# State products on half of the rows, and 64- and 32-wide attention tiles

## The chip, the core and the metric

One core of a Trainium2 chip runs the whole program in one launch. The metric is the device time in microseconds (us); smaller is better. Before the change the median of 3 runs is 1411.97 us (1411.93 to 1413.6). The profile is of one further execution, which took 1415.93 us.

## The reference

Three stages follow each other. `B, H, S, Ns, D` are 8, 8, 512, 32, 64: batches, heads, tokens, state rows of a head, and the width of a head. `x` and `state` are drawn in fp32, the weights are stored in 64 bits.

```
scores = scale * x @ state.T              # per batch and head: 512 x 32
a      = softmax(scores);   xread = a @ state
scores2 = scale * state @ x.T             # 32 x 512
a2     = softmax(scores2);  sread = a2 @ x
tokens = concat([xread, sread]) -> (8*(512+32)) x 512
h  = ((tokens @ w1) * (tokens @ w2)) @ w3
y  = h @ w_out
out = (sigmoid(y @ w_gate) * (y @ w_val)) @ w_out2
```

Since `xread = a @ state`, the product `xread @ w1` is `a @ (state @ w1)`: the kernel multiplies each head's state with its 64 rows of `w1` and `w2` once, and then uses `a` as the only moving operand of the first feed-forward layer. These state products, the scores and `sread` are what the change touches.

## The kernel before

**Number formats.** Weights arrive as 64-bit words (tile `raw`, 512 KB a load). ScalarE (ACT) and VectorE (DVE) turn them into fp32 (tile `m`, lines 87 to 101). A product of full accuracy is made of three fp32r matmuls: an operand is split into a high part (ACT, line 61) and a low part (DVE or GpSimd (POOL), line 66), and `products` (line 103) issues high by high, and both mixed products. Scores and `sread` use plain fp32 operands instead, and the trace has two matmuls for each such call.

**State products.** The state lies in `bd`, transposed, as block-diagonal pieces: 128 rows are the 64 dimensions of two neighbouring heads, and 128 columns are 2 batches x 2 heads x 32 state rows, half of them zeros by the block structure. `z` (line 285) is filled with zeros, four DMAs on SyncE's queue (SP) put the state in, 16 transposes and four copies make `bd`. `state_split` (line 304) makes the high and low parts `bds`. A `sw_step` (line 337) takes one 128 x 512 block `wh` of `w1` or `w2`, and makes 2 x 3 matmuls into two PSUM tiles `psw`; ACT copies them to `swst` and stores them to `swd` in DRAM. There are 32 steps, in two passes of 16: the first pass is the head of the program (the columns for the first half of the batches); the second, for the other half, is spread over the first layer of t = 1 and t = 2.

**The main loop over t.** Each of the eight t takes one batch (`ffn1`, line 408). Slots 0 to 7 each make a pair of 128 x 512 products `pab` from `a` (tiles `aT`) and `swh`, the split of what `sw_weights` (line 458) reads back from `swd`; slots 8 to 11 make the product `py` with `wp = w3 @ w_out`. Before a slot's matmuls the functions hung into it run: `after` holds the rest of the attention of this batch (`a2t`, `sread`, `sreadt`, lines 231 to 269), `before` the attention of the next batch (`xt`, `scores`, softmax). `w_out`, `w3` and `wp` are prepared in t = 0, so that the stretch has more DVE work.

**What sets the order.** TensorE (PE) runs in the order in which the code is written. The other engines are put in order by a scheduler at build time. `ps_at`, the PSUM pool of the attention, has two buffers, and `psw` uses the four of `ps_main`.

**After 620 us** the second feed-forward stage runs; the change does not touch it.

Of the kernel before, what the change touches and what calls it, by code (L numbers as in the profile page):

```python
# [20 lines left out]
def tile_state_attention__then__gated_ffns(  # L21
# [20 lines left out]
    P = 128  # L42
# [75 lines left out]
    sw_d = dram.tile([2, 2, 2, 2, P, B // 2, 512], F32, name="swd")  # L118
# [19 lines left out]
    bd = keep.tile([P, G, B // 2, P], F32, name="bd")  # L138
# [7 lines left out]
    with tc.manual_schedule(engines={mybir.EngineType.PE}):  # L146
# [13 lines left out]
        def attention(b):  # L160

            b2, bp = divmod(b, B // 2)
# [14 lines left out]
            def scores():  # L177
                t["st"] = at.tile([P, 2, SC * 4, NS], F32, name="st")
                t["e2"] = at.tile([P, 2, S], F32, name="e2")
                m2 = at.tile([P, 2], F32, name="m2")  # L180
                s2 = at.tile([P, 2], F32, name="s2")
                t["r2"] = at.tile([P, 2], F32, name="r2")
                for k in range(2):
                    pt = ps_at.tile([P, 512], F32, tag="at", name="psc")
                    for q in range(2):
                        nc.tensor.matmul(
                            pt[64 * q : 64 * q + 64],
                            bd[:, 2 * k + q, bp, b2 * 64 : b2 * 64 + 64],
                            t["xT"][:, 2 * k + q],
                            start=True,  # L190
                            stop=True,
                        )
                    nc.vector.transpose(out=t["st"][:, k].rearrange("p a n -> p (a n)"), in_=pt)
# [46 lines left out]
            def sread():  # L240
                pt = ps_at.tile([P, 2, P], F32, tag="at", name="psr")
# [10 lines left out]
                t["sr"] = at.tile([P, 2, P], F32, name="sr")  # L252
# [5 lines left out]
            def sreadt():  # L258
                pt = ps_at.tile([P, 2, 2, 2, NS], F32, tag="at", name="psrt")
                for k in range(2):  # L260
                    nc.tensor.transpose(
                        pt[:, k].rearrange("p q h n -> p (q h n)"), t["sr"][:, k], ident
                    )
                xv = p2["xst"].rearrange("p (k q) n -> p k q n", q=2)
                for h2 in range(2):
                    nc.vector.tensor_copy(
                        out=xv[64 * h2 : 64 * h2 + 64, :, :, b * NS : (b + 1) * NS],
                        in_=pt[64 * h2 : 64 * h2 + 64, :, :, h2],
                    )
# [15 lines left out]
        z = p1.tile([P, B // 2, G, 2, D], F32, name="z", bufs=1)  # L285
        nc.vector.memset(z, 0.0)
        for b2 in range(2):
            for h2 in range(2):
                p0 = b2 * 64 + h2 * 32
                nc.sync.dma_start(  # L290
                    out=z[p0 : p0 + NS, :, :, h2, :].rearrange("p b g d -> p (b g) d"),
                    in_=state[b2 * (B // 2) : (b2 + 1) * (B // 2), h2::2].rearrange(
                        "b g n d -> n (b g) d"
                    ),
                )
        for g in range(G):
            pt = ps_main.tile([P, 512], F32, tag="m", name="pt")
            for bp in range(B // 2):
                nc.tensor.transpose(
                    pt[:, bp * P : (bp + 1) * P], z[:, bp, g].rearrange("p a d -> p (a d)"), ident  # L300
                )
            copy("act", bd[:, g].rearrange("p a b -> p (a b)"), pt)

        def state_split(pool, bp0):
            t = [pool.tile([P, G, 2, P], F32R, name=f"bds{i}", bufs=1) for i in range(2)]
            for g in range(G):
                split(t[0][:, g], t[1][:, g], bd[:, g, bp0 : bp0 + 2])
            return t
# [12 lines left out]

        def sw_prep(pool, cvs, save):
            def prep(i):
                c, g = (0, 2, 1, 3)[i // G], i % G
                a, hf = divmod(c, 2)
# [11 lines left out]
        def sw_step(i, bp0, bds, wh, pool):  # L337
            c, g = (0, 2, 1, 3)[i // G], i % G
            a, hf = divmod(c, 2)
            st = pool.tile([P, 2, 512], F32, name="swst", bufs=3 if bp0 == 0 else 2)  # L340
            po = [ps_main.tile([P, 512], F32, tag="m", name="psw") for _ in range(2)]
            products(*[(po[q], [([t[:, g, q] for t in bds], wh)]) for q in range(2)], late=1)
            for q in range(2):
                copy("act", st[:, q], po[q])
            nc.scalar.dma_start(out=sw_d[hf, g % 2, g // 2, a, :, bp0 : bp0 + 2], in_=st)

        order = [q * (B // 2) + bp for bp in range(B // 2) for q in range(2)]
        before, after = attention(order[0])
        bds = state_split(p1, 0)
# [4 lines left out]
        for i in range(2 * JF):  # L354
            sw_step(i, 0, bds, wh(i), p1)
            if i == 0:
                for fn in stages:
                    fn()
        p1.release()
# [98 lines left out]
        def sw_weights(b):  # L458
            b2, bp = divmod(b, B // 2)

            def prep(j):
                f = pb.tile([P, 2, 2, P], F32, tag="swf", name="swf", bufs=3)
                f0 = j % 4 * P
                for q in range(2):
                    nc.sync.dma_start(
                        out=f[64 * q : 64 * q + 64].rearrange("p k a f -> p (k a) f"),
                        in_=sw_d[
                            j // 4, q, :, :, 64 * b2 : 64 * b2 + 64, bp, f0 : f0 + P
                        ].rearrange("k a p f -> p (k a) f"),
                    )  # L470
# [5 lines left out]
                return [[t[i][:, :, a] for i in range(2)] for a in range(2)]  # L476
# [25 lines left out]
        def after_wp():  # L502
# [7 lines left out]
            p2["bds"] = state_split(p2["sw"], 2)  # L510
# [100 lines left out]
        for t, b in enumerate(order):  # L611
# [11 lines left out]
            if 1 <= t <= 2:  # L623
                for i in range(JF):
                    slots[i + 3].append(
                        lambda i=i + (t - 1) * JF: sw_step(i, 2, p2["bds"], p2["wh"](i), p2["sw"])
# [508 lines left out]
```

## Time and profile before

| | us |
|---|---|
| median of 3 runs | 1411.97 |
| the profiled execution | 1415.93 |
| its span | 1414.2 |
| PE busy (matmuls) | 1343.5 |
| weight loads (PEld) | 1145.6 |
| DVE busy | 924.7 |
| ACT busy | 750.2 |
| POOL busy | 278.3 |

PE is busy for 95% of the span, but not evenly: the table of 40 slices on the page shows 5 to 6 tenths in the first two slices (35 us each), 9 in nearly all from the fifth slice on. A busy PE isn't one at its peak, since a matmul's latency counts as busy: what a stretch costs is read from the times at which one group follows the other in the chain that ended last. [...]

### The profile page before, as it was taken

Reading aid. Unit: us, or ns where it says so; the run is one execution under the profiler, and the core shown is the slowest. Engines: PE = TensorE matmul, PEld = TensorE weight load, DVE = VectorE, ACT = ScalarE, POOL = GpSimd, SP = SyncE. Lnnn points to the kernel's source line nnn. Section 1 sums busy time; section 2 is a strip of 40 time slices with the busy share of each in tenths; the row PEclk is TensorE's granted clock in tenths of the full one; section 3 lists DMA queues with packets and bytes.
Section 4 is the critical chain, followed back from the end, with each engine's and each line's share of the span. In section 5 each row is a group of like instructions: output and inputs, shape, how many; then the busy total and the mean of one; then the engine's idle time right before and its main releaser. Section 6 shows DMA issues by size and latency. Waiting matters only on the chain.

```text
span 1414.2 us, 18988 instructions
## 1 busy us (share of the span) xinstructions
PE 1343.5 (95%) x6560; PEld 1145.6 (81%) x6560; DVE 924.7 (65%) x1523; ACT 750.2 (53%) x1480; POOL 278.3 (20%) x255
## 2 busy tenths in 40 slices
PE   5669999999998999999999999999999999999997
PEld 3348877777876777898988998988988888988996
DVE  6789756645555566528677667778777677556543
ACT  6877656756445456436546546545545544433421
POOL 2352113324334234001121121021121110000000
PEclk9889999999999999999999999999999999999999
DMA  9867637754446354383343347655445694134132
GB/s 264 290 195 212 199 135 230 228 195 127 138 119 164 90 155 152 118 319 116 133 151 100 117 165 285 239 183 169 136 167 184 227 324 159 62 108 137 49 104 67
DMA packets 169128, 237.18 MB, mean 168 GB/s; under 512 B 46920, under 2 KB 111944, under 8 KB 166984
## 3 DMA queue, kind: packets, MB, share of 16 engines
q1 hardware_dynamic: 130536, 163.15, 36.6%
q10 hardware_dynamic: 37344, 63.39, 12.8%
q0 software_dynamic: 1152, 9.44, 1.9%
q8 instruction: 51, 0.84, 0.2%
q14 instruction: 45, 0.37, 0.1%
HBM read 150.99 MB, written 84.93 MB: 167 GB/s over the span
## 4 chain that ended last, share of the span: by engine, by line
PE 80%; DVE 6%; issue 5%; DMA 4%; POOL 2%; ACT 2%; ACTq 0%; SPq 0%; DVEq 0%; POOLq 0%
PE po L1019 19%; PE psA L922 18%; PE psB L922 9%; PE pab L112 8%; PE py L112 7%; PE psC L922 5%; PE pab L115 4%; PE py L115 4%; DMA yf<-yd 2%; PE pwp L112 2%; POOL wh L66 2%; PE pwp L115 1%; PE psr L245 1%; PE pxt L170 1%; DMA raw<-in_moe_w 1%
## 5 line engine op out<-in xcount | busy, mean ns | idle before, releaser
L922 PE MATMUL psA<-y,wt 128*128 128x448 f32 (+1 forms) x1440 | 304.6, 360 | 5.6 <-ACT u L61 2.8
L922 PEld LDWEIGHTS psA<-y,wt 128*128 128x128 f32 x1440 | 266.3, 188 | 25.8 <-ACT u L61 3.9
L1019 PE MATMUL po<-wo,p 128*128 128x512 f32 x1224 | 280.7, 389 | 0.4 <-DVE p L590 0.4
L1019 PEld LDWEIGHTS po<-wo,p 128*128 128x128 f32 x1224 | 229.5, 188 | 48.3 <-DVE p L590 1.0
L922 PE MATMUL psB<-y,wt 128*128 128x448 f32 (+1 forms) x720 | 161.1, 359 | 0.0
L66 POOL TENSOR_TENSOR o<-m,o 128x256 fp32r<-128x256 f32 x72 | 59.3, 823 | 503.3 <-ACT o L61 449.1
L112 PE MATMUL pab<-aT,swh 128*128 128x512 f32 x512 | 145.7, 407 | 12.2 <-ACT asb L61 4.7
L922 PEld LDWEIGHTS psB<-y,wt 128*128 128x128 f32 x720 | 133.5, 188 | 8.5
L112 PE MATMUL py<-u,wp 128*128 128x512 f32 (+1 forms) x576 | 132.2, 381 | 2.1 <-DVE u L66 1.7
L61 ACT ACTIVATE u<-psA 128x448 f32<-128x448 f32 (+1 forms) x120 | 63.9, 532 | 127.7 <-PE psA L922 103.0
L112 PEld LDWEIGHTS py<-u,wp 128*128 128x128 f32 x576 | 104.0, 189 | 28.5 <-issue 5.7
L66 POOL TENSOR_TENSOR swh<-swf,swh 128x512 fp32r<-128x512 f32 x64 | 90.8, 1424 | 167.9 <-ACT swh L61 155.0
L112 PEld LDWEIGHTS pab<-aT,swh 128*128 128x128 f32 x512 | 95.3, 193 | 35.0 <-ACT asb L61 6.4
L61 ACT ACTIVATE p<-sg 128x448 fp32r<-128x448 f32 (+1 forms) x120 | 67.9, 566 | 86.6 <-DVE sg L958 79.0
L434 DVE TENSOR_TENSOR asb<-asb,pab 128x512 f32<-128x512 f32 (+1 forms) x72 | 47.0, 654 | 98.8 <-PE pab L115 90.3
L101 DVE CUSTOM_DVE_ANT_0 m<-m,r 128x1024 uint16<-128x1024 uint16 (+1 forms) x116 | 80.1, 692 | 11.1 <-ACT r L90 1.3
L66 DVE TENSOR_TENSOR u<-asb,u 128x512 fp32r<-128x512 f32 (+1 forms) x72 | 65.9, 916 | 30.7 <-ACT u L61 30.1
L1034 DVE TENSOR_TENSOR ob<-po,ob 128x512 f32<-128x512 f32 x68 | 46.8, 688 | 58.7 <-PE po L1019 55.4
L115 PE MATMUL pab<-aT,swh 128*128 128x512 f32 x256 | 81.7, 401 | 2.0 <-POOL swh L66 2.0
L922 PE MATMUL psC<-y,wt 128*128 128x448 f32 (+1 forms) x360 | 80.9, 360 | 1.1 <-DVE s L955 1.1
L61 ACT ACTIVATE y<-yf 128x448 fp32r<-128x448 f32 (+1 forms) x120 | 63.1, 558 | 32.4 <-DMA yf<-yd 32.4
L98 DVE SCALAR_TENSOR_TENSOR m<-raw,m 128x512 uint32<-128x512 uint32 (+1 forms) x116 | 78.2, 676 | 3.2
(118 smaller groups left out, 2028.3 us busy)
## 6 DMA issues: line engine op xcount, KB each, us to landing
raw<-in_moe_w SPq DMA_DIRECT2D x48, 512.0 KB, 5.6
wt<-wd SPq DMA_DIRECT2D x12, 1792.0 KB, 7.6
part<-ob SPq DMA_DIRECT2D x68, 256.0 KB, 2.8
ob<-part SPq DMA_DIRECT2D x68, 256.0 KB, 3.9
yf<-yd SPq DMA_DIRECT2D x37, 448.0 KB, 4.0
swd<-swst ACTq DMA_DIRECT2D x32, 512.0 KB, 4.1
swf<-swd SPq DMA_DIRECT2D x128, 128.0 KB, 3.7
wd<-o ACTq DMA_DIRECT2D x56, 256.0 KB, 2.3
```

Source lines behind the costliest of these rows:

```text
L61: return nc.scalar.activation(out=o, in_=i, func=AF.Copy)
L66: (sub or nc.vector).tensor_tensor(out=lo, in0=src, in1=hi.bitcast(F32), op=ALU.subtract)
L98: nc.vector.scalar_tensor_tensor(out=mu, in0=hi, scalar=0x80000000, in1=mu, op0=ALU.bitwise_and, op1=ALU.bitwise_or)
L101: nc.vector.tensor_tensor(out=m.bitcast(I32), in0=m.bitcast(I32), in1=r, op=ALU.add)
L112: nc.tensor.matmul(o, w[i], xx[k], start=n == 0 and i + k == 0, stop=False)
L115: nc.tensor.matmul(o, w[1 - late], xx[late], start=False, stop=n == len(pairs) - 1)
L170: nc.tensor.transpose(pt[:, c * P : (c + 1) * P], xn[b][:, g, c].rearrange("p a d -> p (a d)"), ident)
L245: nc.tensor.matmul(pt[64 * q : 64 * q + 64, k], t["a2"][:, k, c, 64 * q : 64 * q + 64], xn[b][:, 2 * k + q, c].rearrange("p a d -> p (a d) ...
L434: p2["dve"] = nc.vector.tensor_tensor(out=asb[:, :n], in0=asb[:, :n], in1=pab[1][:, :n], op=ALU.mult)
L922: nc.tensor.matmul(o, w[:, i, kb * P : (kb + 1) * P], xx[kb][h], start=start, stop=i == 1 and kb == 1, skip_group_check=True,)
L1019: nc.tensor.matmul(o, pt[j][i][:, s * P : (s + 1) * P], wot[j][:, h], start=j == js[0] and i + h == 0, stop=j == js[-1] and i == 1,)
L1034: nc.vector.tensor_tensor(out=ob, in0=o, in1=ob, op=ALU.add)
```

## The change

`bd` is replaced by `stT`, the plain transpose of the state: 128 rows are the dimensions of a pair of heads (even head in rows 0 to 63, odd head in rows 64 to 127), and the columns of pair `g` are 8 batches x 32 state rows. No zeros are stored.

- **State products**: the stationary operand of one matmul is 64 rows x 128 columns (four batches x 32 state rows of one head). A step makes 3 x 2 matmuls again, `k` = 0 on rows 0 to 63 into one PSUM tile, `k` = 1 on rows 64 to 127 into the other. The number of steps (32) and of matmuls (192) stays.
- **Scores**: 8 calls instead of 4, each on 64 rows and 32 columns; the two halves `k` go to two PSUM tiles that are both taken at the start.
- **sread**: 32 calls instead of 16, each on 128 rows and 32 columns with 64 moving columns instead of 128.
- **sreadt**: one transpose and one copy instead of two of each.
- **Head**: no zero fill; eight state DMAs, six of them on ACT's queue; 4 transposes and one copy before the first step, the other 4 and one copy after the fifth.
- **DRAM layout** of `swd`: a store writes two runs of 2 KB for each partition instead of one of 4 KB; one DMA of 256 KB instead of two of 128 KB reads a slot's block back. Batches are taken in the order 0 to 7.

```diff
-    sw_d = dram.tile([2, 2, 2, 2, P, B // 2, 512], F32, name="swd")
+    sw_d = dram.tile([2, 2, G, NS, 4, 2, 2, 512], F32, name="swd")
-    bd = keep.tile([P, G, B // 2, P], F32, name="bd")
+    stT = keep.tile([P, G, NSR], F32, name="stT")
...
-                for k in range(2):
-                    pt = ps_at.tile([P, 512], F32, tag="at", name="psc")
-                    for q in range(2):
+                pts = [ps_at.tile([P, 512], F32, tag="at", name="psc") for _ in range(2)]
+                for g in range(G):
+                    for k in range(2):
                         nc.tensor.matmul(
-                            pt[64 * q : 64 * q + 64],
-                            bd[:, 2 * k + q, bp, b2 * 64 : b2 * 64 + 64],
-                            t["xT"][:, 2 * k + q],
+                            pts[k][NS * g : NS * g + NS],
+                            stT[64 * k : 64 * k + 64, g, b * NS : (b + 1) * NS],
+                            t["xT"][64 * k : 64 * k + 64, g],
...
-                        for q in range(2):
+                        for g in range(G):
                             nc.tensor.matmul(
-                                pt[64 * q : 64 * q + 64, k],
-                                t["a2"][:, k, c, 64 * q : 64 * q + 64],
-                                xn[b][:, 2 * k + q, c].rearrange("p a d -> p (a d)"),
+                                pt[NS * g : NS * g + NS, k],
+                                t["a2"][:, k, c, NS * g : NS * g + NS],
+                                xn[b][:, g, c, k],
...
-        z = p1.tile([P, B // 2, G, 2, D], F32, name="z", bufs=1)
-        nc.vector.memset(z, 0.0)
...
+        z = p1.tile([P, 2, H, D], F32, name="z", bufs=1)
+        for b in range(B):
+            (nc.sync if b in (1, 3) else nc.scalar).dma_start(
+                out=z[b % 4 * NS : b % 4 * NS + NS, b // 4],
+                in_=state[b].rearrange("h n d -> n h d"),
+            )
...
+        def state_split(pool, h4):
+            t = [pool.tile([P, G, P], F32R, name=f"sts{i}", bufs=1) for i in range(2)]
+            for g in range(G):
+                v = [i[:, g].rearrange("p (n b) -> p b n", b=4) for i in t]
+                split(*v, stT[:, g, h4 * P : (h4 + 1) * P].rearrange("p (b n) -> p b n", b=4))
+            return t
...
-            products(*[(po[q], [([t[:, g, q] for t in bds], wh)]) for q in range(2)], late=1)
+            for m, (x, w) in enumerate(((0, 0), (1, 0), (0, 1))):
+                for k in range(2):
+                    nc.tensor.matmul(
+                        po[k],
+                        sts[x][64 * k : 64 * k + 64, g],
+                        wh[w][64 * k : 64 * k + 64],
+                        start=m == 0,
+                        stop=m == 2,
+                    )
```

On PE, in slot 4 of t = 1 (`psr` is `sread`, `psw` a state step, `pab` the first layer; in a row the calls stand, the width of the output's partitions x its columns), before:

```order
L115 MATMUL pab<-aT_1665,swh_1737 128x512 x2
L245 MATMUL psr<-xn,a2tr 64x128 x16
L112 MATMUL psw<-wh_1819,bds_1487 128x512
L112 MATMUL psw<-wh_1819,bds_1488 128x512
L112 MATMUL psw<-wh_1819,bds_1487 128x512
L112 MATMUL psw<-wh_1819,bds_1488 128x512
L115 MATMUL psw<-wh_1820,bds_1487 128x512 x2
L112 MATMUL pab<-aT_1665,swh_1770 128x512
```

and now:

```order
L115 MATMUL pab<-aT_1667,swh_1738 128x512 x2
L246 MATMUL psr<-xn,a2tr 32x64 x32
L344 MATMUL psw<-wh_1819,sts_1490 128x512 x2
L344 MATMUL psw<-wh_1819,sts_1491 128x512 x2
L344 MATMUL psw<-wh_1820,sts_1490 128x512 x2
L112 MATMUL pab<-aT_1667,swh_1770 128x512
```

The place of the groups is the same; `psr` has twice the calls, and the six calls of `psw` now alternate between the two row halves, while they went tile by tile before.

On PE, in slot 8 of t = 1 (`psc` are the scores of the next batch, `py` the second product), before:

```order
L115 MATMUL pab<-aT_1665,swh_1981 128x512 x2
L112 MATMUL psw<-wh_2020,bds_1487 128x512
L112 MATMUL psw<-wh_2020,bds_1488 128x512
L112 MATMUL psw<-wh_2020,bds_1487 128x512
L112 MATMUL psw<-wh_2020,bds_1488 128x512
L115 MATMUL psw<-wh_2021,bds_1487 128x512 x2
L186 MATMUL psc<-xT,bd 64x512 x4
```

and now:

```order
L115 MATMUL pab<-aT_1667,swh_1994 128x512 x2
L344 MATMUL psw<-wh_2031,sts_1490 128x512 x2
L344 MATMUL psw<-wh_2031,sts_1491 128x512 x2
L344 MATMUL psw<-wh_2032,sts_1490 128x512 x2
L185 MATMUL psc<-xT,stT 32x512 x8
```

The scores have eight calls instead of four, right behind a state step.

On ACT, from the start of the program, before:

```order
L89 ACT_TABLE_LOAD
L89 ACTIVATE m<-raw 128x512
L90 ACTIVATE r<-raw 128x512
L89 ACTIVATE m<-raw 128x512
L90 ACTIVATE r<-raw 128x512
L61 ACTIVATE wh_151<-m 128x512
L61 ACTIVATE wh_164<-m 128x512
L61 ACTIVATE bd<-pt 128x512
L89 ACTIVATE m<-raw 128x512
L61 ACTIVATE bd<-pt 128x512
L61 ACTIVATE bds_132<-bd 128x256 x2
L61 ACTIVATE bd<-pt 128x512 x2
```

and now:

```order
L282 DMA z<-in_state 32x8x64 x6
L61 ACT_TABLE_LOAD
L61 ACTIVATE stT<-pt 128x4x128
L89 ACTIVATE m<-raw 128x512
L61 ACTIVATE sts_117<-stT 128x4x32 x4
L90 ACTIVATE r<-raw 128x512
L89 ACTIVATE m<-raw 128x512
L90 ACTIVATE r<-raw 128x512
L89 ACTIVATE m<-raw 128x512
L61 ACTIVATE wh_136<-m 128x512
```

Six DMA issues come first, the state's copy and its four halved splits stand ahead of the weights' conversion instead of behind it, and three of the four `bd` copies are gone from this place (one comes back after the fifth step).

## Rows read from the trace of the kernel before

**Rows 1.** The page, part 1: busy time and share of each engine.

```profile
PE 1343.5 (95%) x6560; PEld 1145.6 (81%) x6560; DVE 924.7 (65%) x1523; ACT 750.2 (53%) x1480; POOL 278.3 (20%) x255
```

**Rows 2.** Busy time of each engine by stretch (stretch, its length, engines, clock, DMA).

```profile
core 0: us, PE busy (x) PEld busy (x) DVE busy (x) ACT busy (x) POOL busy (x), PEclk, DMA share, GB/s
...
40.00:70.00 30.00, 21.56 (x57) 12.43 (x57) 20.89 (x26) 24.38 (x46) 12.71 (x10) 0.81 0.88 296
70.00:110.00 40.00, 27.75 (x112) 19.68 (x113) 34.01 (x41) 28.91 (x53) 21.63 (x16) 0.83 0.70 197
...
190.00:330.00 140.00, 137.89 (x677) 110.21 (x676) 80.60 (x110) 87.14 (x159) 42.16 (x31) 1.00 0.57 183
330.00:440.00 110.00, 108.52 (x570) 86.89 (x569) 62.60 (x87) 59.20 (x106) 42.17 (x35) 1.00 0.47 140
```

**Rows 3.** The chain that ended last, in t = 3 (start, length, what).

```profile
333.49 1.90 PE psr L245 x32
335.38 1.12 PE pab L112 x4
...
336.97 0.91 PE pab L112 x4
...
341.06 0.22 PE psrt L261 x2
...
349.44 1.87 PE psc L186 x8
351.31 3.89 PE py L112 x16
...
357.02 3.63 PE py L112 x16
```

**Rows 4.** The same chain in t = 1, a state step.

```profile
215.46 0.91 PE psw L112 x4
216.37 0.45 PE psw L115 x2
```

**Rows 5.** Weight loads in order of time around one batch's scores (start, length, what).

```profile
511.64 0.14 PEld L186 LDWEIGHTS psc<-xT,bd 128*64 128x64 f32 x2 [0.28 <-issue]
512.07 0.14 PEld L186 LDWEIGHTS psc<-xT,bd 128*64 128x64 f32 x2 [0.29 <-issue]
```

**Rows 6.** All matmuls of scores and of sread (durations in ns: least, median, most).

```profile
L186 PE MATMUL psc<-xT,bd x64: 592/592/643, 19.6 to 512.5; 128*64 128x512 f32 x64
...
L245 PE MATMUL psr<-xn,a2tr x256: 272/273/476, 107.4 to 548.6; 128*64 128x128 f32 x128
```

**Rows 7.** ACT in order of time in the head's steady part.

```profile
55.20 0.63 ACT L61 ACTIVATE wh<-m 128x512 fp32r<-128x512 f32 x1 [0.58 <-DVE m L101]
...
56.85 1.08 ACT L61 ACTIVATE swst<-psw 128x512 f32<-128x512 f32 x2
```

**Rows 8.** All engines in order of time, the first 15 us.

```profile
0.74 0.87 SPq L80 DMA_DIRECT2D raw<-in_moe_w  x2
...
3.03 1.93 SPq L290 DMA_DIRECT2D z<-in_state  x4
...
11.57 0.60 ACT L61 ACTIVATE bd<-pt 128x512 f32<-128x512 f32 x1 [0.50 <-PE pt L299]
...
13.09 0.72 ACT L61 ACTIVATE bds<-bd 128x256 fp32r<-128x256 f32 x2
...
13.74 1.53 PE L112 MATMUL psw<-wh,bds 128*128 128x512 f32 x4
```

**Rows 9.** The chain in t = 1, from the scores to the next slots.

```profile
231.12 1.03 PE psc L186 x4
...
256.21 6.30 DMA raw<-in_moe_w
...
269.94 1.20 PE pab L112 x4
```

**Rows 10.** The chain in t = 5, a pause of PE.

```profile
445.07 5.88 issue
```

More of the change, by code (lines that the diff above doesn't have):

```diff
@@ L251, in sread @@
                             )
-                t["sr"] = at.tile([P, 2, P], F32, name="sr")
+                t["sr"] = at.tile([P, 2, D], F32, name="sr")
                 for k in range(2):
@@ L258, in sreadt @@
             def sreadt():
[L259 to L269, printed above, removed]
+                pt = ps_at.tile([P, G, NS], F32, tag="at", name="psrt")
+                nc.tensor.transpose(
+                    pt.rearrange("p g n -> p (g n)"), t["sr"].rearrange("p k d -> p (k d)"), ident
+                )
+                nc.vector.tensor_copy(out=p2["xst"][:, :, b * NS : (b + 1) * NS], in_=pt)
             before = {
@@ L284, in tile_state_attention__then__gated_ffns, with state_turn @@
         tc.swap_default_side()
-        z = p1.tile([P, B // 2, G, 2, D], F32, name="z", bufs=1)
-        nc.vector.memset(z, 0.0)
[L287 to L294, printed above, removed]
-                )
[L296 to L308, printed above, removed]
+        z = p1.tile([P, 2, H, D], F32, name="z", bufs=1)
[4 more added lines that the diff above has]
+            )
+        def state_turn(h4):
+            pt = ps_main.tile([P, 512], F32, tag="m", name="pt")
+            for g in range(G):
+                nc.tensor.transpose(
+                    pt[:, g * P : (g + 1) * P],
+                    z[:, h4, 2 * g : 2 * g + 2].rearrange("p a d -> p (a d)"),
+                    ident,
+                )
+            copy("act", stT[:, :, h4 * P : (h4 + 1) * P], pt.rearrange("p (g m) -> p g m", g=G))
+        state_turn(0)
         def ahead(prep, depth, count):
@@ L320, in ahead, with sw_tile @@
             return take
+        def sw_tile(i):
+            hf, r = divmod(i, 2 * G)
+            return (hf, *divmod(r, 2))
         def sw_prep(pool, cvs, save):
             def prep(i):
-                c, g = (0, 2, 1, 3)[i // G], i % G
-                a, hf = divmod(c, 2)
+                hf, g, a = sw_tile(i)
                 wf = cvt((w1, w2)[a][g * P : (g + 1) * P, hf * 1024 : (hf + 1) * 1024], cvs[i % len(cvs)])
@@ L335, in sw_prep, with sw_step @@
             return ahead(prep, 2, 2 * JF)
[L337 to L340, printed above, removed]
-            po = [ps_main.tile([P, 512], F32, tag="m", name="psw") for _ in range(2)]
-            products(*[(po[q], [([t[:, g, q] for t in bds], wh)]) for q in range(2)], late=1)
[L343 to L347, printed above, removed]
+        def state_split(pool, h4):
+            t = [pool.tile([P, G, P], F32R, name=f"sts{i}", bufs=1) for i in range(2)]
+            for g in range(G):
+                v = [i[:, g].rearrange("p (n b) -> p b n", b=4) for i in t]
+                split(*v, stT[:, g, h4 * P : (h4 + 1) * P].rearrange("p (b n) -> p b n", b=4))
+            return t
+        def sw_step(i, h4, sts, wh, pool):
+            hf, g, a = sw_tile(i)
+            st = pool.tile([P, 2, 512], F32, name="swst", bufs=3 if h4 == 0 else 2)
+            po = [ps_main.tile([P, 512], F32, tag="m", name="psw") for _ in range(2)]
+            for m, (x, w) in enumerate(((0, 0), (1, 0), (0, 1))):
+                for k in range(2):
+                    nc.tensor.matmul(
[4 more added lines that the diff above has]
+                        stop=m == 2,
+                    )
+            for k in range(2):
+                copy("act", st[:, k], po[k])
+            nc.scalar.dma_start(
+                out=sw_d[h4, hf, g, :, :, a].rearrange("n b k f -> (n b) (k f)"),
+                in_=st.rearrange("p k f -> p (k f)"),
+            )
+        order = list(range(B))
         before, after = attention(order[0])
-        bds = state_split(p1, 0)
+        sts = state_split(p1, 0)
         wh = sw_prep(p1, (cv, p1), False)
@@ L354, in tile_state_attention__then__gated_ffns @@
         for i in range(2 * JF):
-            sw_step(i, 0, bds, wh(i), p1)
+            sw_step(i, 0, sts, wh(i), p1)
             if i == 0:
@@ L358, in tile_state_attention__then__gated_ffns @@
                     fn()
+            if i == G:
+                state_turn(1)
         p1.release()
@@ L463, in prep @@
                 f0 = j % 4 * P
[L464 to L470, printed above, removed]
+                nc.sync.dma_start(
+                    out=f.rearrange("p a k f -> p (a k) f"),
+                    in_=sw_d[b // 4, j // 4, :, :, b % 4, :, :, f0 : f0 + P].rearrange(
+                        "g n a k f -> (g n) (a k) f"
+                    ),
+                )
                 t = [
@@ L475, in prep @@
                 split(t[0], t[1], f, sub=nc.gpsimd)
-                return [[t[i][:, :, a] for i in range(2)] for a in range(2)]
+                return [[t[i][:, a] for i in range(2)] for a in range(2)]
             return ahead(prep, 2, JF)
@@ L509, in after_wp @@
             p2["wh"] = sw_prep(p2["sw"], (cv,), True)
-            p2["bds"] = state_split(p2["sw"], 2)
+            p2["sts"] = state_split(p2["sw"], 1)
         def open_wst():
@@ L625, in tile_state_attention__then__gated_ffns @@
                     slots[i + 3].append(
-                        lambda i=i + (t - 1) * JF: sw_step(i, 2, p2["bds"], p2["wh"](i), p2["sw"])
+                        lambda i=i + (t - 1) * JF: sw_step(i, 1, p2["sts"], p2["wh"](i), p2["sw"])
                     )
```

5 lines of the change are left out of this document (2 added, 3 removed).

## The prediction

> **What bounds the kernel now.** First the busy times: PE is busy for 1343.5 us of the 1414.2 us span and every other engine for 65% or less [rows 1], so PE time is worth something where PE isn't waiting. Where that is, the busy times by stretch show [rows 2]. From 190 to 330 us PE is busy for 137.9 of 140 us, from 330 to 440 for 108.5 of 110. Before 110 us it is not the bound: from 40 to 70 us PE is busy for 21.6 of 30 us at a mean clock of 0.81 and ACT for 24.4; from 70 to 110 us PE for 27.8 of 40 and DVE for 34.0. In the order of time ACT runs there without a pause except for some 0.6 us before each `wh`, where it waits for DVE [rows 7]. So there are three places to look at: the head (to 70 us), bound by ACT; the start of t = 0 (to 110 us), bound by DVE; and t = 0 to 7 from there to about 620 us, bound by PE. Of the second feed-forward stage nothing changes.
>
> Next, what the touched groups cost in the PE-bound part is read from the chain, where one group's start is the other's end. A state step takes 0.91 + 0.45 = 1.36 us for 6 matmuls, 0.227 each [rows 4]. In t = 3 `psr` takes 1.90, `psc` 1.87 and two `psrt` 0.22 us [rows 3]. Behind `psr` the first four `pab` take 1.12 instead of 0.91, behind `psc` the first sixteen `py` take 3.89 instead of 3.63 [rows 3]: 0.21 and 0.26 us for coming back from narrow tiles to the full array.
>
> How much of the array works there? The scores are four calls, and the trace has eight matmuls for them. Their weight loads come in twos, 0.43 us apart [rows 5]; four such turns are 1.72 of the 1.87 us. One of these matmuls lasts 592 ns [rows 6]. As in a stream at the granted clock one matmul of 512 columns and one pass needs 0.227 [rows 4], 0.43 is two passes, and two matmuls run side by side, on the two halves of 64 columns. For `psr` the same holds: 32 matmuls in 16 turns of 0.109 us are 1.74 of 1.90 us. What is left, 0.15 us, and the 0.21 or 0.26 us behind it are the price of one visit to the narrow tiles, about 0.40 us.
>
> **The change part by part**, against the profiled execution of 1415.93 us.
>
> *State steps in t = 1 and 2.* 16 of the 32 steps lie there. No row shows matmuls on row halves, so the price has two ends. If the halves run side by side, as column halves do, a step is 3 turns of 0.227 = 0.68 us, and if they take turns it stays at 1.36. The step now needs a visit of its own, 0.40 us, which it did not need before; four of the 16 stand next to `psr` or `psc` and share one border (some 0.2 us less). So between 16 x (0.68 + 0.40 - 1.36) - 0.8 = -5.3 us and 16 x 0.40 - 0.8 = +5.6 us. I take -4.8, near the first: the nearest row is that of the column halves [rows 5]; the rest is for weight loads, now 128 columns wide when a visit begins, not 64.
>
> *Scores.* 8 calls, 16 matmuls, on 8 tiles (2 row halves x 4 strips of 32 columns). Side by side on all eight: 2 turns of 0.43 instead of 4, -0.86 us, and some 0.03 us to start eight one after another: -0.83. With only two at a time: 8 turns, +1.72. Seven of eight batches' scores lie in the PE-bound part (the first lies in the head): -5.8, or up to +12.0. I take -5.8.
>
> *sread.* 32 calls, 64 matmuls, each with half the moving columns, on 4 strips. A turn is half of 0.109, and 64 / 4 = 16 turns are 0.87 instead of 1.74 us: -0.87 at best. It can also cost: in no row does PE run more than 32 matmuls in 1.74 us, one every 54 ns. If that is as fast as they can be handed to the array, 64 of them take 3.49 us, +1.74. I take -0.75, near the best end, since the weight loads of the two tiles of one turn start together, and the turns are as long as two passes need, which explains the 54 ns without any other limit [rows 5, 6]. Seven lie in the PE-bound part: -5.2. That of t = 0 lies where DVE sets the pace.
>
> *sreadt.* One transpose less, half of 0.22 us, seven times: -0.8. One `xst` copy less on DVE is hidden under PE.
>
> *What does not get through.* In t = 1 the chain leaves PE at the scores (231.12) and comes back to it only at 269.94, through the softmax on DVE and a load of `raw` of 6.30 us [rows 9]. PE is busy meanwhile, but waits at its end: what PE saves in between (three state steps and the gain of the scores, 3 x 0.3 + 0.83) is waited for there. +1.7.
>
> *Head.* ACT makes four `bd` copies of 0.60 us and four `bds` splits of 0.36, 3.8 us [rows 8]. After: two copies, 1.2 us, and four splits of half the size, which I put by the line through 512 columns (0.60) and 256 (0.36) at 0.24 each: 2.2 us. ACT sets the pace of the head, so -1.6. The zero fill and the z DMAs behind it (issued at 3.03) leave DVE and SP early on; instead two z DMAs stand ahead of the first `raw` on SP (+1.0 us by 1.93 / 4 each [rows 8]), and six on ACT's queue, where ACT still waits for data. The first state step (13.74) waits for the splits now; without them it would be due about 1 us after its weights. Ends: +1.5 (the late `raw` moves everything) and -4. PE has its state steps halved there as well, and that is hidden: `swst` waits for ACT's own turn [rows 7]. [...]
>
> *DMA.* 64 fewer issues on SP and runs of 2 KB instead of 4 KB in `swd`: nothing, SP and the DMA queues (share 0.5 to 0.6 from 190 to 330 us) aren't on PE's path.
>
> *Sum*: -4.8 - 5.8 - 5.2 - 0.8 + 1.7 - 1.6 = -16.5 us. The profiled execution would take 1399.4 us; it stands 4.0 us above the median of the runs, so the median is forecast at 1411.97 - 16.5 = 1395.5 us.
>
> **The rivals.**
>
> *A. The forecast*: all tiles work side by side. 1395.5, within 1390 to 1401.
>
> *B. The rate at which matmuls are handed to the array sets `psr`* (the other side). Twice as many matmuls as before, each half as long, gain only where one can start every 14 ns on average; from 27 ns on `psr` gains nothing, and from about 50 ns on the whole change is a loss. At the densest rate in the trace, 54 ns, `psr` goes from 1.74 to 3.49 us: seven times 2.49 us more than in A, and once about 1.7 in t = 0: 1395.5 + 19.1 = 1414.6 us. For it: no denser row. Against it: the array's own time explains the 54 ns.
>
> [...]
>
> *C. Row halves take turns, column strips don't.* State steps +5.6 instead of -4.8, the scores keep 4 turns (0 instead of -5.8): 1395.5 + 16.2 = 1411.7, no change. For it: no row with row halves. Against it: nothing but the likeness to column halves.
>
> *D. PE's saving is eaten by the others.* About 1.7 us go from each t (0.83 + 0.75 + 0.11), some 2.4 more from t = 1 and 2, and ACT, DVE, POOL and the loads must follow; in t = 1 and 2 ACT is busy for 87 of 140 us and DVE for 81, and the path of rows 9 shows that they are late at times. If half of the 15 us is lost in such waits: 1403 to 1406.
>
> *E. More goes than PE's time.* In t = 5 PE pauses for 5.88 us [rows 10], because a transpose waits for a PSUM buffer which DVE, held up, empties late. Another phase between the engines, and one copy instead of two, may take it away, or the head may gain 4 us: 1388. Such a pause may as well appear elsewhere, which is in A's upper edge.
>
> **How the numbers follow.** A 0.55, B 0.08, C 0.08, D 0.14, E 0.15. The likeliest gives 1395.5. The range goes from 1385 (E, with both of its gains) to 1408 (D and its upper edge); B and C are left out, 0.16, and little else. About 2.8 us, 0.2%, is what a measurement of this kernel can tell from no change: below 1409.1 are A, D, E and a small part of C, 0.85; C's rest is no change, with the edges of D and B, 0.07; B is slower, 0.08.
>
> **What would show each step.** In the profile after: `psc` near 1.0 us and `psr` near 1.1 in the chain in t = 3, with weight loads of eight and four tiles close together; a state step near 1.1 us in t = 1, with two matmuls starting together, and the `pab` group behind it some 0.2 us longer than 0.91; each t from 3 on about 1.7 us shorter; the first `pab` of t = 0 some 1.6 us earlier. `psr` above 1.9 us would mean B, a state step of 1.7 us C, and PE waits in t = 1 to 7 summing to more than 10 us D. The forecast is wrong if tiles don't run side by side by eights, or if a pause like that of t = 5 comes more than once.

## The result, and the profile after

The changed kernel takes 1398.39 us (median of 4 runs, 1396.00 to 1401.08) against 1411.95 (1409.89 to 1413.60) for the kernel before on the same chip: a ratio of 0.9905, 95% interval 0.9883 to 0.9928. Forecast were 1395.5 us and a range of 1385 to 1408, so the direction and the range held; the gain is 13.6 us instead of 16.5. The profiled executions are 1415.93 us (span 1414.2) before and 1398.74 us (span 1397.0) after, 17.2 us apart; that of before lies 4.0 us above its first median of 1411.97.

Where these 17.2 us come from is read by following the first matmul of a few groups through both traces:

| first matmul of | before, us | after, us | moved since the row above |
|---|---|---|---|
| `pab` in t = 0 | 75.0 | 81.5 | +6.4 |
| `psr` in t = 0 | 107.4 | 113.8 | 0 |
| `psr` in t = 1 | 209.2 | 219.0 | +3.4 |
| `psr` in t = 3 | 333.4 | 334.2 | -9.0 |
| `psr` in t = 5 | 436.8 | 433.4 | -4.2 |
| `psr` in t = 6 | 495.2 | 483.0 | -8.8 |
| `psr` in t = 7 | 546.9 | 532.6 | -2.1 |
| `psA` (second stage) | 620.6 | 604.0 | -2.3 |
| end of the span | 1414.2 | 1397.0 | -0.6 |

So the head and t = 0 lost 9.8 us where a small gain was forecast, and t = 1 to 7 won 26.4.

The busy times of the profile of after, answering to [rows 1] (busy us, share, instructions):

```profile
PE 1317.5 (94%) x6864; PEld 1115.1 (80%) x6864; DVE 917.2 (66%) x1514; ACT 744.5 (53%) x1478; POOL 280.6 (20%) x255
```

The same stretches as in [rows 2], after (columns as there):

```profile
40.00:70.00 30.00, 16.24 (x51) 7.04 (x51) 21.59 (x28) 23.96 (x44) 11.26 (x8) 0.50 0.81 274
70.00:110.00 40.00, 24.43 (x86) 15.60 (x86) 30.82 (x35) 27.50 (x51) 21.73 (x17) 0.80 0.69 221
190.00:330.00 140.00, 137.19 (x793) 102.80 (x779) 81.98 (x117) 88.89 (x166) 42.26 (x31) 0.99 0.60 196
330.00:440.00 110.00, 108.99 (x701) 87.76 (x700) 65.80 (x90) 63.10 (x116) 46.16 (x38) 1.00 0.48 148
```

TensorE is still the bound from 190 us on. From 40 to 70 us its granted clock, as a share of full speed, is 0.50, where it was 0.81 on average.

The chain in t = 3, answering to [rows 3], and two rows of t = 1, answering to [rows 4] (start, length, what):

```profile
334.24 1.03 PE psr L246 x64
335.27 1.13 PE pab L112 x4
...
340.94 0.12 PE psrt L261
...
349.02 1.02 PE psc L185 x16
350.04 3.87 PE py L112 x16
...
355.72 3.63 PE py L112 x16
```

```profile
215.23 0.90 PE psw L344 x6
216.12 1.13 PE pab L112 x4
```

The weight loads of a batch's scores [rows 5] now stand sixteen in a row, for eight tiles and two passes; the matmuls themselves are as long as before [rows 6], only more of them run at once:

```profile
348.95 0.18 PEld L185 LDWEIGHTS psc<-xT,stT 64*32 64x32 f32 x16 [0.35 <-issue]
```

```profile
L185 PE MATMUL psc<-xT,stT x128: 589/613/1061, 25.2 to 498.3; 64*32 64x512 f32 x128
```

`psr` went from 1.90 to 1.03 us, `psc` from 1.87 to 1.02, `psrt` from 0.22 to 0.12. A state step is 0.90 us and 0.22 for the border behind it (1.13 instead of 0.91), together 1.12 instead of 1.36.

### The profile page after: what moved, and what is told of

It is laid out like the page before. It is cut to its first block, busy times and chain, and to the rows that moved or that the text cites. A ratio compares the mean times of both kernels' runs of the same rounds, so it can differ in the third digit from the quotient of the medians.

```text
span 1397.0 us, 19437 instructions
## 1 busy us (share of the span) xinstructions
PE 1317.5 (94%) x6864; PEld 1115.1 (80%) x6864; DVE 917.2 (66%) x1514; ACT 744.5 (53%) x1478; POOL 280.6 (20%) x255
## 4 chain that ended last, share of the span: by engine, by line
PE 78%; DVE 6%; DMA 5%; issue 5%; ACT 3%; POOL 2%; SPq 1%; ACTq 0%; DVEq 0%; POOLq 0%
PE po L1029 18%; PE psA L932 18%; PE psB L932 9%; PE pab L112 8%; PE py L112 8%; PE psC L932 5%; PE pab L115 4%; PE py L115 4%; PE pwp L112 1%; POOL wh L66 1%; DMA yf<-yd 1%; DMA raw<-in_moe_w 1%; DMA ob<-part 1%; PE psw L344 1%; DVE y L600 1%
## 5 line engine op out<-in xcount | busy, mean ns | idle before, releaser
L61 ACT ACTIVATE u<-psA 128x448 f32<-128x448 f32 (+1 forms) x120 | 63.7, 531 | 129.4 <-PE psA L932 103.9
L447 DVE TENSOR_TENSOR asb<-asb,pab 128x512 f32<-128x512 f32 (+1 forms) x72 | 47.0, 654 | 80.1 <-PE pab L115 72.2
L101 DVE CUSTOM_DVE_ANT_0 m<-m,r 128x1024 uint16<-128x1024 uint16 (+1 forms) x116 | 76.6, 662 | 15.1 <-ACT r L90 4.6
L89 ACT ACTIVATE m<-raw 128x512 f32<-128x512 f32 (+1 forms) x116 | 65.7, 568 | 29.6 <-POOL o L66 15.4
```

The costliest lines, as they stand in the source:

```text
L61: return nc.scalar.activation(out=o, in_=i, func=AF.Copy)
L89: nc.scalar.activation(out=m, in_=hi.bitcast(F32), func=AF.Abs, scale=2.0**-112)
L101: nc.vector.tensor_tensor(out=m.bitcast(I32), in0=m.bitcast(I32), in1=r, op=ALU.add)
L447: p2["dve"] = nc.vector.tensor_tensor(out=asb[:, :n], in0=asb[:, :n], in1=pab[1][:, :n], op=ALU.mult)
```

## Experiments: do the tiles run side by side, and why

*onehalf* takes the row halves away: both head groups' state products are made on the upper half.

```
-  sts[x][64 * k : 64 * k + 64, g],   wh[w][64 * k : 64 * k + 64],
+  sts[x][0:64, g],                   wh[w][0:64],
```

> The state products of both head groups are made on the upper row half (the lower half's operands are left out, so these products are not the reference's); nothing else differs. Theory 1, the gain of a state step comes from the two row halves running side by side: on one half the six matmuls take turns, 6 times 0.227 = 1.36 us and a visit's border, 1.4 to 1.6 us a step, the 16 steps in t = 1 and 2 cost 8 to 11 us more, 1406 to 1410 us. Theory 2, a matmul on 64 rows is itself shorter: 0.90 us a step as now, 1397 to 1400 us.

Measured: 1407.57 us (1406.38 to 1409.74), ratio 0.9949 (0.9928 to 0.9969). The chain in t = 1:

```profile
214.97 1.59 PE psw L344 x6
216.55 1.12 PE pab L112 x4
```

Six turns of 0.23 us and a border: theory 1. A matmul on 64 rows is no shorter here (three more turns cost 1.59 - 0.90 = 0.69 us, 0.23 each) than one on 128 (0.227 [rows 4]); the gain comes from the halves running at the same time. Of 16 x 0.69 = 11.0 us more TensorE time in t = 1 and 2, 9.2 arrive in the median.

*kmajor* and *gouter* keep the work and change the order of the calls on the tiles.

```
-  for m, (x, w) in enumerate(...):          # state step
-      for k in range(2):
+  for k in range(2):
+      for m, (x, w) in enumerate(...):
```

> A state step's six matmuls in another order: the three of the upper row half first, then the three of the lower half, instead of in turn. Theory 1, matmuls are handed out in the order of the program with hardly any look ahead, and halves run side by side only because they stand side by side in the program: a step goes from 0.90 to between 1.1 and 1.36 us (five or six turns of 0.227), the 16 steps of t = 1 and 2 cost 3 to 7 us more, 1401 to 1406 us. [...]

```
-  for k in range(2):                        # sread
-      for c in range(SC):
-          for g in range(G):
+  for g in range(G):
+      for k in range(2):
+          for c in range(SC):
```

> sread with the strips outermost: the sixteen matmuls of one strip of 32 columns follow each other in the program, then those of the next strip; the work is the same. Theory 1 (hardly any look ahead): the strips take turns, 64 times 0.055 us, psr 3.5 us instead of 1.03; seven batches lie where TensorE sets the pace, 1414 to 1417 us. [...]

Measured: kmajor 1396.91 us (1395.20 to 1397.62), ratio 0.9874 (0.9857 to 0.9892), a step as long as with the change (0.90 us), so theory 1 falls there. gouter 1411.36 us (1408.23 to 1416.99), ratio 0.9986 (0.9971 to 1.0001): nearly the whole gain is gone. A step of kmajor in the chain, and `psr` of gouter in t = 3 in order of time:

```profile
214.28 0.90 PE psw L344 x6
215.18 1.13 PE pab L112 x4
```

```profile
342.84 3.18 PE L246 MATMUL psr<-xn,a2tr 128*32 128x64 f32 x64
345.95 1.19 PE L112 MATMUL pab<-aT,swh 128*128 128x512 f32 x4
```

`psr` takes 345.95 - 342.84 = 3.11 us, three times the 1.03 of the change and less than the 3.5 of theory 1, which in its pure form falls here too; the time is below its range. The starts of the single matmuls show how far the strips overlap. The sixteen of a strip come every 0.056 us, and the next strip's first start comes when three of the strip before are still due (us from the first start, next strip's in brackets; the records don't name the strip, so this is told by the two even spacings):

```
0.639  0.695  [0.700]  0.750  [0.780]  0.806  [0.836]  0.862  [0.892]  [0.948]
```

Without overlap 64 matmuls take 64 x 0.0558 = 3.57 us; at each of the three borders between strips three of them, 0.17 us, lie beside others: 3.57 - 3 x 0.17 = 3.07 us, close to 3.11. Of 7 x (3.11 - 1.03) = 14.6 us, 13.0 arrive in the median. In kmajor the lower half's first call stands behind three on the other tile, and a step takes 0.90 us, as with the change's own order, where calls change tiles each time. So what counts seems to be the run of calls on one tile: in gouter the next strip starts with three of the strip before still due, and the sum fits if that holds at each of the three borders. Runs of other lengths than one, three and sixteen were not tried.

So the starts in this trace don't keep to the order of the program: the next strip's first matmul starts at 0.700, ahead of three that stand before it (0.750, 0.806 and 0.862).

## Experiments: the head

*The first three* kernels move the state's loads; *headbusy* gives TensorE its work back.

```
 zhalf:       state of batches 0-3 first, 4-7 on SP behind load_x
 zafter:      three weight tiles, all state on SP, then load_x
 zafter_half: three weight tiles, state 0-3, load_x, state 4-7
 headbusy:    -  for ... in enumerate(((0, 0), (1, 0), (0, 1))):
              +  first product (0, 0) three times where h4 == 0
```

> Only the state of batches 0 to 3 (four transfers, two on each of the two queues) is issued at the start; that of batches 4 to 7 goes on SyncE's queue behind the loads of the first batch's x. Question: why does t = 0 start 6.4 us later with the change (first pab at 81.46 instead of 75.03 us)? Theory 1, the state's transfers stand ahead of the weights, so that the raw tiles, and ScalarE's conversions behind them, are late: with half of them gone the first pab comes at 76 to 78 us and the kernel takes 1393 to 1396 us. Theory 2, TensorE's lower granted clock in the head (0.50 from 34 to 85 us) sets it: no change, first pab at 81 to 82 us, 1398 us.

> The first three weight tiles are issued ahead of everything on SyncE's queue, then all eight state transfers on the same queue, then x; ScalarE converts the weights before it evicts the turned state. Theory 1 (transfers ahead of the weights): the first wh comes at 9 us as before the change, the first pab at 73 to 75 us, the kernel takes 1390 to 1392 us. Theory 2 (the lower clock): first pab at 81 us, 1398 us. A third: the state, now last, makes the first state step late (after 20 us) and the head gains nothing, 1397 to 1400 us.

> Weight tiles first on SyncE's queue, then the state of batches 0 to 3, x, and the state of batches 4 to 7. Theory 1 (transfers ahead of the weights): as zafter, and up to 1 us better since x is not behind the second half of the state: first pab at 72 to 75 us, 1389 to 1392 us. Theory 2 (the lower clock): first pab at 81 us, 1398 us.

> The first product of each state step in the head is made three times (ten matmuls a step instead of six; the result is the same), so that TensorE is about as busy there as before the change. Theory 2 (the lower granted clock sets the head): the clock from 34 to 85 us comes back to about 0.8, the first pab comes at 76 to 78 us, the kernel takes 1393 to 1395 us. Theory 1 (transfers): first pab at 81 to 82 us, the time 1397 to 1400 us whatever the clock does.

| | first `pab`, us | median, us (runs) | ratio, 95% |
|---|---|---|---|
| after | 81.5 | 1398.39 (1396.00 to 1401.08) | 0.9905 (0.9883 to 0.9928) |
| zhalf | 80.1 | 1396.64 (1396.02 to 1398.09) | 0.9893 (0.9878 to 0.9908) |
| zafter | 81.1 | 1396.79 (1393.45 to 1398.70) | 0.9890 (0.9872 to 0.9908) |
| zafter_half | 80.8 | 1396.79 (1393.36 to 1398.39) | 0.9887 (0.9867 to 0.9907) |
| headbusy | 82.0 | 1399.18 (1397.26 to 1401.56) | 0.9910 (0.9895 to 0.9926) |

Theory 1, transfers ahead of the weights, misses the first `pab` by 2 us in zhalf and by 6 in the other two. zafter's third theory, a first state step later than 20 us, fails too: ScalarE empties that step from 17.25 us on. The differences in the table are small: three other kernels with the head of after (gouter, twocopies, swf2) have their first `pab` between 80.7 and 81.9 us. Theory 2, the clock, isn't supported, but headbusy is a weak test of it: the clock came up only in the first part (busy times as in [rows 2]):

```profile
34.00:55.00 21.00, 12.63 (x54) 8.43 (x54) 15.77 (x21) 13.71 (x25) 5.54 (x4) 0.61 0.65 231
55.00:85.00 30.00, 20.81 (x79) 12.79 (x78) 19.28 (x24) 22.78 (x42) 12.33 (x10) 0.50 0.85 282
```

With both theories short, the order of ScalarE's instructions was read. Before, in order of time:

```profile
15.85 1.10 ACT L61 ACTIVATE swst<-psw 128x512 f32<-128x512 f32 x2
16.80 0.67 ACT L61 ACTIVATE wh<-m 128x512 fp32r<-128x512 f32 x1
...
18.36 0.68 ACT L89 ACTIVATE m<-raw 128x512 f32<-128x512 f32 x1
```

and after:

```profile
14.79 0.63 ACT L61 ACTIVATE wh<-m 128x512 fp32r<-128x512 f32 x1
20.61 0.66 ACT L89 ACTIVATE m<-raw 128x512 f32<-128x512 f32 x1 [5.18 <-DMA raw<-in_moe_w]
21.17 0.62 ACT L61 ACTIVATE wh<-m 128x512 fp32r<-128x512 f32 x1
21.69 1.07 ACT L61 ACTIVATE swst<-psw 128x512 f32<-128x512 f32 x2
```

The conversion of the fourth weight tile now stands ahead of the first state step's eviction. ScalarE waits 5.18 us for that tile, the eviction behind it comes at 21.69 us instead of 15.85, and the first batch's scores are late. In zhalf the scores are early again, but the same conversion stands behind the exponentials of the first batch and starts at 26.61 us. Where the loads stand in the program seems to have changed the order that the scheduler gives to ScalarE; so the next kernel asks for a place that restores the old order.

*zlate*:

```
+ load_z(range(4))                 # at the start; 4-7 in the loop:
+ if i == 3: load_z(range(4, 8))
- if i == G: state_turn(1)
+ if i == 2 * G: state_turn(1)
```

> As zhalf, but the state of batches 4 to 7 is asked for behind the fourth state step, and turned in the ninth instead of the fifth. That also puts ScalarE's conversions of the fourth to sixth weight tile ahead of the exponentials of the first batch, where they stood before the change (in zhalf they stand behind them; with the change as it is, the fourth stands ahead of the first state step's eviction). Theory 3, the order of ScalarE's instructions in the head sets when t = 0 starts: first pab at 75 to 77 us, 1391 to 1394 us. Theory 4, the head is paced by its transfers (weights and products share the DMA engines), in whatever order ScalarE works: first pab at 79 to 81 us as in the three kernels with other places for the state, 1396 to 1397 us.

Measured: 1389.85 us (1389.17 to 1393.20), ratio 0.9831 (0.9811 to 0.9851), first `pab` at 76.2 us: theory 3, with a time 1 us below its range. It beats the change (its interval lies wholly below) as well as the kernel before. Its rows:

```profile
15.17 1.07 ACT L61 ACTIVATE swst<-psw 128x512 f32<-128x512 f32 x2
...
18.87 0.67 ACT L89 ACTIVATE m<-raw 128x512 f32<-128x512 f32 x1
```

Its clock is as low as in after (0.50 from 30 to 75 us; after 0.50 from 34 to 85 us), so the clock isn't what cost the 5.3 us that came back.

That still is no gain over 75.0, though ScalarE has some 1.5 us less to do (two `stT` and four `sts` instructions take 2.3 us, 3.8 before [rows 8]). VectorE's first instruction on the scores is late; before, after, zlate:

```profile
20.70 0.72 DVE L193 STREAM_TRANSPOSE st<-psc 128x512 f32<-128x512 f32 x1 [0.48 <-PE psc L186]
```

```profile
27.92 0.72 DVE L194 STREAM_TRANSPOSE st<-psc 128x512 f32<-128x512 f32 x1
```

```profile
22.25 0.72 DVE L194 STREAM_TRANSPOSE st<-psc 128x512 f32<-128x512 f32 x1 [0.66 <-PE psc L185]
```

The first `pab` follows 54.3, 53.5 and 53.9 us later, so zlate's 1.2 us against before lie ahead of the scores. Two things are late there. ScalarE's first conversion of a weight tile, whose load now stands behind two state loads, before and in zlate:

```profile
5.53 0.66 ACT L89 ACTIVATE m<-raw 128x512 f32<-128x512 f32 x1 [3.51 <-DMA raw<-in_moe_w]
```

```profile
7.80 0.66 ACT L89 ACTIVATE m<-raw 128x512 f32<-128x512 f32 x1 [4.81 <-DMA raw<-in_moe_w]
```

By the first eviction (15.85 and 15.17 us, above) ScalarE has made that good. The scores themselves come next, before and in zlate:

```profile
19.57 1.94 PE L186 MATMUL psc<-xT,bd 128*64 128x512 f32 x8 [0.40 <-ACT xT L61]
```

```profile
19.59 2.56 PE L185 MATMUL psc<-xT,stT 64*32 64x512 f32 x16
```

They start together. But by the diff the first of the two PSUM tiles needed two of the four `xT` pieces before, and both need all four now: VectorE could start at 20.70 us, with the second tile still in work, and starts at 22.25 us, when all is done. No kernel separates this from the rest of the 1.5 us. And from 22 to 38 us VectorE, third in the row, is busy for nearly all 16 us, before and in zlate:

```profile
22.00:38.00 16.00, 10.11 (x29) 5.90 (x27) 15.77 (x24) 11.18 (x22) 4.85 (x3) 0.79 0.80 302
```

```profile
22.00:38.00 16.00, 7.45 (x37) 3.57 (x30) 15.56 (x25) 11.52 (x22) 4.98 (x3) 0.71 0.84 289
```

*dvemore* and *actmore* add work to zlate on one engine or the other.

```
 dvemore: + nc.vector.transpose of the softmax weights twice, batch 0
 actmore: + both exponentials e2 twice, batch 0
```

> zlate with one more instruction on VectorE in the head: the first batch's transposition of the weights of attention (1.25 us) is made twice. Question: which engine sets the pace of the head up to 40 us, where the change took 1.6 us off ScalarE and nothing was gained? Theory 1, VectorE (in zlate it works without a pause from the first scores at 22.25 to 38.4 us): first pab 1.0 to 1.3 us later than in zlate, 77.2 to 77.5 us. Theory 2, ScalarE, as the prediction had it: first pab within 0.4 us of zlate's 76.2 us.

> zlate with two more instructions on ScalarE in the head: the first batch's two exponentials (0.69 us each, and 0.19 for each of their sums) are made twice, 1.76 us more of ScalarE between 24 and 29 us. Theory 1, VectorE sets the pace there: first pab within 0.5 us of zlate's 76.2 us. Theory 2, ScalarE does: first pab 1.5 to 1.8 us later, 77.7 to 78.0 us.

Measured: dvemore has its first `pab` at 77.0 us, 0.8 later than zlate and just short of theory 1's range; 1393.50 us (1390.75 to 1395.94), ratio 0.9862 (0.9843 to 0.9881). actmore has it at 75.8 us, 0.4 earlier; 1391.70 us (1390.67 to 1392.72), ratio 0.9848 (0.9832 to 0.9864). But the scores don't come at the same time in the three kernels; VectorE's first instruction on them in dvemore and in actmore:

```profile
21.79 0.72 DVE L194 STREAM_TRANSPOSE st<-psc 128x512 f32<-128x512 f32 x1 [0.78 <-PE psc L185]
```

```profile
21.16 0.71 DVE L194 STREAM_TRANSPOSE st<-psc 128x512 f32<-128x512 f32 x1
```

Counted from there the first `pab` follows 55.2 us later in dvemore, 1.3 more than zlate's 53.9, and 54.6 in actmore, 0.7 more. In after, gouter, twocopies and swf2, whose heads are alike, this count is 53.5 to 53.6 us, so it is steady enough to be read. VectorE's 1.25 us more arrive in full, ScalarE's 1.76 us to less than half: VectorE is the nearer bound from 22 to 38 us, as theory 1 has it, but ScalarE isn't free there. In actmore VectorE waits for it at the last step before `pab`:

```profile
35.27 1.23 DVE L66 TENSOR_TENSOR aT<-a2tr,aT 128x1024 fp32r<-128x1024 f32 x1 [1.13 <-ACT aT L61]
```

## Experiments: the pause that went

Each t from 3 to 6 takes 49.6 us after, t = 5 included; TensorE's pause there [rows 10] is gone. *twocopies* and *swf2* each put one possible cause back.

```
 twocopies: xst copied in two halves of 64 partitions
 swf2:      + for q in range(2): nc.sync.dma_start(out=f[64 * q : 64 * q + 64]...
```

> The change, with the copy into xst made in two halves of 64 partitions again, as before the change. Question: what took away TensorE's pause of 5.88 us in t = 5 (from one psr to the next it took 58.4 us there, 51.7 in the other t; with the change 49.6 in all)? Theory 1, the one copy instead of two, which empties the PSUM buffer sooner: with two the pause comes back in one t, 4 to 7 us, and the kernel takes 1402 to 1405 us. Theory 2, another phase between the engines, not the copies: every t from 3 on stays at 49.5 to 49.9 us, 1396 to 1400 us.

> The change, with each swf tile loaded by two transfers of 64 partitions again, as before the change (64 more issues on SyncE). Before the change the wait behind the pause in t = 5 began with a late swf. Theory 1, the fewer issues on SyncE's queue took the pause away: with two transfers a tile it comes back in one t, 4 to 7 us, 1402 to 1405 us. Theory 2, another phase: every t from 3 on stays at 49.5 to 49.9 us, 1396 to 1400 us.

Measured: twocopies 1400.01 us (1394.60 to 1403.08), ratio 0.9899 (0.9868 to 0.9930), every t from 3 to 6 at 49.8: no pause, so the two copies alone don't bring it back. (From `psr` of t = 7 to `psA` it takes 3.3 us longer than after, but at a mean clock of 0.95 instead of 1.00, and TensorE is idle there for 2.6 us instead of 2.3.) swf2 1401.26 us (1399.88 to 1402.14), ratio 0.9919 (0.9904 to 0.9935), with 52.3 us for t = 5 and 50.1 for t = 6: a pause is back in the same t, 3.2 us where 4 to 7 were expected. Its interval overlaps with that of the change, so the reading rests on one trace. SyncE's issues of four `swf` tiles (first row) and a wait of ScalarE or TensorE (the rows behind), before the change:

```profile
432.16 11.74 SPq L465 DMA_DIRECT2D swf<-swd  x8
```

```profile
440.64 0.63 ACT L61 ACTIVATE swh<-swf 128x512 fp32r<-128x512 f32 x1 [3.23 <-DMA swf<-swd]
```

in swf2:

```profile
423.68 11.84 SPq L476 DMA_DIRECT2D swf<-swd  x8
```

```profile
432.26 0.63 ACT L61 ACTIVATE swh<-swf 128x512 fp32r<-128x512 f32 x1 [3.31 <-DMA swf<-swd]
```

```profile
438.82 0.66 PE L169 MATMUL pxt<-ident,xn 128*128 128x128 f32 x4 [3.23 <-DVE xst L264]
```

and after:

```profile
428.81 8.06 SPq L475 DMA_DIRECT2D swf<-swd  x4
```

Four tiles stand on SyncE's queue for 11.7 us as eight transfers and for 8.1 as four. With eight, ScalarE's `swh` waits 3.2 to 3.3 us; what stands behind it on ScalarE and VectorE, the `xst` copy last, empties the PSUM buffer late, and TensorE's transposes wait. The same chain stands in both traces with two transfers a tile, and in none of the other kernels was a t from 3 to 6 longer than the next by over 0.3 us. Why TensorE lost 5.88 us before and 3.23 in swf2 stays open. Before, t = 5 is 6.7 us longer than its neighbours and not 5.88: TensorE's granted clock, 1.00 until the pause, is 0.51 from 447.4 to 454.2 us, in the pause and behind it.

## Why the prediction was right, and where it was not

*Scores, sread, sreadt*: right. Forecast -0.83, -0.75 and -0.11 us a t; measured -0.85, -0.87 and -0.10 in the chain of t = 3, with borders as before. The 0.03 us put in for eight starts, one after another, was an estimate that no row shows; after the change the eight tiles of `psc` start within 0.047 us. A t is 2.1 us shorter, not 1.7; these three make 1.8 of it, and TensorE's waits at the transposes `pxt` fall from 0.7 to 0.5 us.

*State steps*: the mechanism right, 0.90 us and 0.22 for the border against 0.68 and 0.40: -0.24 x 16 = -3.8 us, and less where a step shares its border with `psr` or `psc`. The term was -4.8.

*The lost wait in t = 1* (+1.7): not settled. From `psr` of t = 1 to that of t = 2 it took 63.7 us before and takes 59.0, as if no wait were left; but t = 0 is longer by 3.4 us. The two together take 165.5 us before, 164.2 after, and 164.0, 163.5 and 163.9 in zlate, dvemore and actmore, whose head isn't late. Only 1.3 to 2.0 us are won there, where the terms forecast about 5.0 without the lost wait (0.9 in t = 0, and 1.7 and half the state steps, 2.4, in t = 1) and 3.3 with it. So more was lost than forecast, with a late head or an early one, and which wait took it isn't shown.

*t = 0* (no term of its own): +3.4 us. TensorE's clock goes with it, but not alone. From `psr` of t = 0 to that of t = 1, in before, after, zlate, dvemore and actmore (columns as in [rows 2]):

```profile
107.40:209.20 101.80, 99.61 (x499) 80.82 (x498) 74.32 (x122) 64.75 (x119) 17.91 (x13) 0.99 0.62 182
```

```profile
113.80:219.00 105.20, 99.76 (x537) 79.83 (x536) 75.12 (x121) 64.28 (x119) 17.86 (x13) 0.97 0.56 171
```

```profile
108.50:211.20 102.70, 98.04 (x536) 78.55 (x535) 75.20 (x122) 64.33 (x119) 17.78 (x13) 0.99 0.57 175
```

```profile
109.30:214.20 104.90, 99.72 (x539) 79.75 (x538) 75.12 (x122) 64.36 (x119) 17.88 (x13) 0.97 0.57 171
```

```profile
108.10:212.80 104.70, 99.62 (x536) 79.65 (x535) 75.24 (x122) 64.23 (x119) 17.84 (x13) 0.97 0.56 171
```

Of these the three at a mean of 0.97 are the long ones. In after the granted clock is 0.51 from 205.0 to 208.4 us, behind 5 us in which TensorE was busy for 3.07. But zafter takes 104.4 us at 1.00, and swf2 101.1 at 1.00, so the clock isn't all of it, and no kernel tests it. ScalarE's order in the head isn't the cause either: dvemore and actmore have the old one. The cause stays open.

*Head* (-1.6): wrong in sign, +6.4 us. The step that failed is "ACT sets the pace of the head, so -1.6". It was read from 40 to 70 us and carried back to the first 15 us, where the saved copies lie. There the saving made good a late `raw` (7.80 us instead of 5.53) and showed in the first eviction (15.17 us in zlate, 15.85 before); but t = 0 starts 54 us behind the first scores, and these came later, not earlier. From there to 38 us VectorE is the nearer bound (dvemore, actmore). The upper end, +1.5 for a late `raw`, named the right object and missed the larger cause: the order of ScalarE's instructions, worth 5.3 us of the head. The prediction compared the order of work on TensorE; of ScalarE's it had the first rows, and not those from the first eviction on.

*DMA* ("nothing"): wrong in the good direction. The pause of t = 5 went, 6.7 us of the profiled execution, and with two loads a tile 3.2 of them come back (swf2), so the 64 fewer issues on SyncE are at least part of the cause. Rival E had the pause go by another phase or by the one copy; twocopies speaks against the copy. Whether the other executions of the kernel before have the pause isn't recorded; the profiled one lies 4.0 us above the median.

*Rivals.* B fell: 64 matmuls of `psr` start within 0.88 us, 13.8 ns each, where 54 ns had been the densest. gouter comes near B's figure in another way, 1411.4 against 1414.6 us. C fell by 0.90 us a step and by onehalf. D fell: between the `psr` of t = 1 and `psA` TensorE is idle for 11.6 us before and 5.2 after.

So the forecast of 1395.5 came near 1398.4 partly by luck: two misses of opposite sign, head with t = 0 (+9.8 where -1.6 was forecast) and t = 5 (-6.7 where nothing was), partly cancel. With the head in its old order the kernel takes 1389.85.

## What to carry to other kernels

Here small matmuls on different tiles of the array ran side by side where calls changed tiles after one or three (`psr` from 1.90 to 1.03 us, `psc` from 1.87 to 1.02, a state step's six calls in 0.90 us in both orders); with runs of sixteen on one tile, as in gouter, `psr` took 3.11 us, and nearly the whole gain was gone. A change of loads seems able to reorder an engine's whole queue where a scheduler decides it: compare the order of every engine that sets a pace, not only of the one that was edited, and ask for each stretch anew which one that is. Fewer, larger transfers are worth counting even where their queue isn't on the path: four tiles held SyncE's queue for 11.8 us in eight transfers (swf2) and for 8.1 in four (after).

## What was not expected of the hardware

Eight tiles start 6 to 7 ns apart (0.047 us from the first to the eighth of `psc`), though each call makes two passes, one behind the other, on its own tile (the second passes start from 0.454 us on). In gouter the next strip's first matmul starts at 0.700 us, ahead of the last three of the strip before it, which stand ahead of it in the program. The price of a visit to narrow tiles did not grow with their number here: 1.03 - 0.88 + 0.22 = 0.37 us for `psr` on four strips, and 1.90 - 1.74 + 0.21 = 0.37 on two halves before. And TensorE at a granted clock of 0.50 for 45 us (zlate, 30 to 75 us; before, 0.80) cost nothing that could be seen where VectorE and ScalarE set the pace: from the first scores to the first `pab` it took 53.9 us, and 54.3 before.
